# A fused attention and two-MLP kernel: the second MLP's combined weights are made during the first MLP

## The chip, the cores and the metric

The kernel runs on one core of a Trainium2 chip. The metric is the device time of one execution in microseconds (us), shown as the median of several runs. Five engines work in parallel and each takes its instructions in order: PE (matrix multiply, with its weight loads shown as PEld), DVE (vector), ACT (activations and copies), POOL (GpSimd) and SP, whose queue only issues DMAs here.

## The reference

```python
# decayed linear attention: B=4, H=8, S=768, D=48
state = alpha[:, :, t, :, None] * state + k[:, :, t] (outer) v[:, :, t]
y[:, :, t] = q[:, :, t] @ state
x = y as (3072 tokens, 384)
# first MLP, d_ff = 2048
x = silu(x @ w_in) @ w_out
# second MLP, d_ff = 1536
out = (silu(x @ w_gate) * (x @ w_val)) @ w_out2
```

Everything is float32. Weights arrive as 64-bit floats, and the kernel turns them into float32 itself: that is what `decode` does, with three integer operations on DVE (L47, L52, L57) on a tile of 128x384 words. A float32 product is formed as three PE products: each operand is split into a rounded high part (an ACT copy, `high_...`) and a low part (source minus high, `sub`, L267), and PE adds high*high, low*high and high*low.

## The kernel before

**First MLP with attention.** The 24 chunks of 128 tokens are put in seven blocks of 4, 3, 3, 3, 3, 4 and 4 chunks. For each block j the kernel runs 16 steps, one for each 128 rows of the hidden layer. A step has two half steps: `g1` makes the hidden row block (9 matmuls, L648 to L651), `act1` has ACT apply silu twice (L665, L666) and DVE form the low part `gl` (L267), and `g2` adds the row block's share of the output (9 matmuls, L682 to L685). `g1` of the next step is issued ahead of `g2` of this one. `slot` is called after each half step and interleaves the attention of the next block: `qkt` and `pt` for a pair of heads, `pv` for a finished chunk. At the end of a chunk's attention the rows go to the next block's input tile `x`, part of them by small DMAs (`rows_in`, L552), and at the end of a block `g2` stores the result `x1e` to DRAM (L694). Blocks 0 and 1 are interleaved; blocks 2 to 6 follow one another. In the profile block 2 begins at 200 us, block 6 at 483 us, and the first MLP ends at 546.4 us.

**Second MLP.** The 3072 tokens are three pairs of 512-token halves. For a pair, `group(p, u)` runs for u = 0..11 and multiplies 2x2 blocks with fewer products than the direct way: the moving operand is 9 prepared combinations of the tokens (`mov`, made by `moving_steps`), the stationary operand is 9 prepared combinations of four 128x128 weight blocks (`comb`, a high and a low half, 128 x 18 x 128 floats). A group has 33 matmuls (L827), and between them ACT copies (L861, L863, L876), silu (L842) and DVE additions and products (L867, L882, L845). Then the output stage of the pair runs: for each of 24 tiles `osplit` makes a high part on ACT and a low part `al` (DVE, and POOL for half of them in pair 0), and `og` issues 9 matmuls (L909) with the output weights `wo`.

**Making comb and wo.** One combined weight u takes two loads from DRAM (384 KB each, raw), two decodes (six DVE operations), four POOL operations on 128x128 (`combine`, L796 to L799), an ACT copy of 128x1152 (`high_comb`, L803), a POOL subtraction of 128x1152 (`low_comb`, L267) and a DMA store to `comb_d` (`keep_comb`, L810). Pairs 1 and 2 fetch it from there (`fetch_comb`, L814); pair 0 uses it where it was made. One wo takes one load, three DVE operations, an ACT copy (L818) and a POOL subtraction of 128x384. `units2` advances all of these by at most one item per stage; it is called from the last half steps of block 5, from most half steps of block 6, and inside pair 0 from the groups (`spare`, twice in even groups) and the output stage. A decode there is three DVE operations in a row.

**What sets the order.** The order on every queue is the order of the calls above. The tiles `big0`, `big1`, `big2` hold the blocks' inputs and results in turn.

Of the kernel before, what the change touches and what calls it, by code (L numbers as in the profile page):

```python
# [222 lines left out]
def fast(ctx, tc, pk, w1, w2, out, bad_i):  # L223
# [24 lines left out]
    mp = ctx.enter_context(tc.tile_pool(name="mp", bufs=2))  # L248

# [49 lines left out]
    def load_in(n, part=None):  # L299
# [416 lines left out]
    def moving_steps(p):  # L716
# [16 lines left out]
        def minus(out, x, y):  # L733
            POOL.tensor_tensor(out=out, in0=x, in1=y, op=ALU.subtract)
# [25 lines left out]
    f_t, comb_t, wo_t, loaded, ticks = {}, {}, {}, {}, [0]  # L760

    def comb_place(u):
        t = pools2["s"].tile([128, 18 * 128], F32R, tag=f"comb{u % 3}", name=f"comb{u}", bufs=1)
        comb_t[u] = t.rearrange("p (x i e) -> p x i e", x=2, i=9)
        return t
# [12 lines left out]
    def decode2(w):
        key = "2", w
        decode_unit(key, 0)  # L780
        decode_unit(key, 1)
        if w >= 2 * NF2:
            return decode_unit(key, 2)
        u, i = divmod(w, 2)
        if i == 0:
            f_t[u] = pools2["s"].tile([128, 10, 128], F32, tag="f", name=f"f{u}", bufs=2)
        to = f_t[u][:, 3 * (1 - i):3 * (1 - i) + 3].rearrange("p k e -> p (k e)")
# [13 lines left out]
    def high_comb(u):  # L801
        comb_place(u)
        ACT.activation(out=comb_t[u][:, 0], in_=f_t[u][:, 1:], func=AF.Copy)  # L803

    def low_comb(u):
        t = comb_t[u]
        sub(POOL, t[:, 1], f_t[u][:, 1:], t[:, 0])

    def keep_comb(u):
        SP.dma_start(out=comb_d[u], in_=comb_t[u].bitcast(F32).rearrange("p x i e -> p (x i e)"))  # L810

    def fetch_comb(u):
# [39 lines left out]
    def group(p, u, spare):  # L852
# [16 lines left out]
        if u % 2 == 0:  # L869
            spare()  # L870
# [23 lines left out]
    def osplit(p, f, b):  # L894
# [5 lines left out]
        sub(POOL if p == 0 and b else DVE, al, a, ah)  # L900
# [27 lines left out]
    st = dict.fromkeys(("a1", "a2", "a3", "b", "c", "gd", "qk", "pv", "end", "l1", "d1", "e1", "f1", "h1", "s1", "l2", "f2", "c2", "h2", "s2", "sp", "hw", "sw"), 0)  # L928
# [90 lines left out]
    def units2(room=3):  # L1019

        was = dict(st)
        ticks[0] += 1

        def step(key, limit, fn):
            if was[key] < limit:
                fn(st[key])
                st[key] += 1

        step("sp", was["s2"], keep_comb)
        step("s2", was["h2"], low_comb)  # L1030
        step("sw", was["hw"], low_wo)
        step("h2", min(was["c2"], room), high_comb)
        if "r" in pools2:
            step("hw", was["f2"] - NW, high_wo)
# [289 lines left out]
```

## Time and profile before

| | us |
|---|---|
| median of 3 runs | 1012.17 |
| lowest and highest run | 1011.71, 1014.96 |
| time of the profiled execution | 1011.36 |
| span of the profiled execution | 1009.6 |
| PE busy | 960.6 |
| DVE busy | 532.3 |
| ACT busy | 431.1 |
| POOL busy | 278.7 |

The span runs from the first to the last instruction; 1.76 us of the profiled time lie around it. Busy times are sums over an engine's instructions; a matmul's recorded duration overlaps with the next one's.

### The profile page before, as it was taken

The numbers are of one execution on the slowest core, as the hardware profiler recorded it, in microseconds if no ns is written. First come the engines' busy times: TensorE is split into PE (matmuls) and PEld (weight loads), VectorE is DVE, ScalarE is ACT, GpSimd is POOL, SyncE is SP. The second block draws the span as 40 slices with busy tenths as digits, with TensorE's granted clock in tenths as the row PEclk, the third lists the DMA queues.
The fourth block names the chain that finished last, engine by engine and source line by source line (L and its number), as shares of the span: only waits on it lengthen the run. The fifth ranks groups of instructions, "written<-read, shape, count | busy, mean of one in ns | idle before, by whom it ended". The sixth has DMA issues, their size and how long they took to land.

```text
span 1009.6 us, 14182 instructions
## 1 busy us (share of the span) xinstructions
PE 960.6 (95%) x5317; PEld 808.6 (80%) x5317; DVE 532.3 (53%) x912; ACT 431.1 (43%) x977; POOL 278.7 (28%) x347
## 2 busy tenths in 40 slices
PE   8889999999999999999999998879999999999995
PEld 5667798799999999888787776658788888788884
DVE  7889936444344453543842687793234354343432
ACT  3544435545454554452434444434343343433332
POOL 5344416423142342420630255374100020000000
PEclk9999999999999999999999999989999999999998
DMA  7763102322122222102820358460236410344001
GB/s 233 264 246 98 50 1 97 95 75 74 47 74 65 66 85 65 60 11 79 291 101 31 141 170 284 141 234 1 110 140 237 154 48 32 125 159 169 1 1 66
DMA packets 32780, 111.54 MB, mean 110 GB/s; under 512 B 3648, under 2 KB 7232, under 8 KB 28096
## 3 DMA queue, kind: packets, MB, share of 16 engines
q1 hardware_dynamic: 32224, 110.11, 31.8%
q8 instruction: 43, 0.70, 0.3%
q10 hardware_dynamic: 480, 0.46, 0.2%
q14 instruction: 33, 0.27, 0.1%
HBM read 85.00 MB, written 23.59 MB: 108 GB/s over the span
## 4 chain that ended last, share of the span: by engine, by line
PE 73%; DVE 13%; issue 5%; ACT 3%; POOL 3%; DMA 2%; SPq 0%; DVEq 0%; POOLq 0%; ACTq 0%
PE u L827 14%; PE o L909 13%; PE p L827 8%; PE h L648 5%; PE h L649 5%; PE h L651 5%; PE x L682 5%; PE x L683 5%; PE x L685 5%; DVE dec L47 3%; DVE raw L52 2%; PE y L489 2%; PE y L511 2%; POOL w L267 2%; DVE a L845 1%
## 5 line engine op out<-in xcount | busy, mean ns | idle before, releaser
L827 PE MATMUL u<-mov,comb 128*128 128x512 f32 x756 | 186.3, 392 | 12.5 <-ACT u L863 9.1
L827 PEld LDWEIGHTS u<-mov,comb 128*128 128x128 f32 x756 | 140.8, 188 | 47.4 <-ACT u L863 12.4
L909 PE MATMUL o<-ah,wo 128*128 128x512 f32 x432 | 136.4, 397 | 0.5 <-ACT ah L899 0.5
L267 DVE TENSOR_TENSOR gl<-h,gh 128x384 fp32r<-128x384 f32 (+1 forms) x112 | 68.6, 612 | 113.9 <-ACT h L666 110.7
L682 PE MATMUL x<-gh,w 128*128 128x384 f32 (+1 forms) x336 | 122.2, 364 | 2.5 <-ACT gh L665 2.5
L648 PE MATMUL h<-x,w 128*128 128x384 f32 (+1 forms) x336 | 122.9, 366 | 1.7 <-DMA x<-y 1.6
L683 PE MATMUL x<-gh,w 128*128 128x384 f32 (+1 forms) x336 | 121.4, 361 | 0.0
L665 ACT ACTIVATE gh<-h 128x384 fp32r<-128x384 f32 (+1 forms) x112 | 59.8, 534 | 144.4 <-PE h L651 144.0
L649 PE MATMUL h<-x,w 128*128 128x384 f32 (+1 forms) x336 | 121.1, 360 | 0.0
L827 PE MATMUL p<-mov,comb 128*128 128x512 f32 x432 | 111.9, 394 | 1.7 <-DVE a L845 1.7
L909 PEld LDWEIGHTS o<-ah,wo 128*128 128x128 f32 x432 | 83.2, 193 | 18.3 <-ACT ah L899 0.9
L827 PEld LDWEIGHTS p<-mov,comb 128*128 128x128 f32 x432 | 81.5, 189 | 20.2 <-DVE a L845 2.9
L909 PE MATMUL o<-al,wo 128*128 128x512 f32 x216 | 87.0, 403 | 7.7 <-DVE al L267 7.4
L685 PE MATMUL x<-gl,w 128*128 128x384 f32 (+1 forms) x336 | 85.5, 362 | 4.1 <-DVE gl L267 4.1
L651 PE MATMUL h<-x,w 128*128 128x384 f32 (+1 forms) x336 | 84.6, 360 | 0.0
L267 DVE TENSOR_TENSOR al<-a,ah 128x512 fp32r<-128x512 f32 x60 | 45.4, 757 | 70.6 <-ACT ah L899 68.2
L899 ACT ACTIVATE ah<-a 128x512 fp32r<-128x512 f32 x72 | 45.4, 630 | 82.4 <-PE o L909 73.8
L356 POOL TENSOR_TENSOR kq<-in,r 128x256 f32<-128x256 f32 x47 | 35.4, 753 | 156.2 <-DVE r L345 152.3
L682 PEld LDWEIGHTS x<-gh,w 128*128 128x128 f32 x336 | 63.5, 189 | 10.7 <-ACT gh L665 5.3
L685 PEld LDWEIGHTS x<-gl,w 128*128 128x128 f32 x336 | 60.7, 188 | 13.5 <-DVE gl L267 7.8
L648 PEld LDWEIGHTS h<-x,w 128*128 128x128 f32 x336 | 63.1, 188 | 10.5 <-issue 5.3
L458 DVE TENSOR_TENSOR pt<-s,mask 128x256 f32<-128x256 f32 x92 | 38.1, 418 | 60.3 <-PE s L435 59.1
(130 smaller groups left out, 1546.9 us busy)
## 6 DMA issues: line engine op xcount, KB each, us to landing
comb<-comb_d SPq DMA_DIRECT2D x24, 1152.0 KB, 5.1
raw<-in_w_dram SPq DMA_DIRECT2D x64, 384.0 KB, 4.8
in<-in_pk_dram SPq DMA_DIRECT2D x22, 770.5 KB, 4.2
comb_d<-comb SPq DMA_DIRECT2D x12, 1152.0 KB, 6.7
in_v<-in_pk_dram SPq DMA_DIRECT2D x24, 256.0 KB, 3.2
x1r<-x_d SPq DMA_DIRECT2D x6, 768.0 KB, 7.5
out_dram<-ob SPq DMA_DIRECT2D x18, 256.0 KB, 2.3
x_d<-x1e SPq DMA_DIRECT2D x4, 576.0 KB, 3.2
```

The source lines that it names most:

```text
L267: eng.tensor_tensor(out=lo, in0=src, in1=hi.bitcast(F32), op=ALU.subtract)
L458: DVE.tensor_tensor(out=pt, in0=s_t[g][0], in1=mask.rearrange("p (o t) -> p o t", o=1).to_broadcast([128, 2, C]), op=ALU.mult,)
L648: PE.matmul(acc, part(u, k), xh, start=(k == 0), stop=False)
L649: PE.matmul(acc, part(u, k, 1), xh, start=False, stop=False)
L651: PE.matmul(acc, part(u, k), xl, start=False, stop=(k == len(xk) - 1))
L665: ACT.activation(out=gh, in_=hb, func=AF.Silu)
L682: PE.matmul(x1_t[j][m], part(u, m), gh, start=(f == 0), stop=False)
L683: PE.matmul(x1_t[j][m], part(u, m, 1), gh, start=False, stop=False)
L685: PE.matmul(x1_t[j][m], part(u, m), gl, start=False, stop=(f == NF1 - 1))
L827: PE.matmul(acc, s[:, hs, i], x[:, hx], start=start and n == 0, stop=n == 2, skip_group_check=True,)
L899: ACT.activation(out=ah, in_=a, func=AF.Copy)
L909: PE.matmul(o_t[b][m], part(wo_t[f], m, l), x, start=(f == 0 and n == 0), stop=(f == NF2 - 1 and n == 2),)
```

## The change

The whole making of the combined weights leaves `units2` and goes to a new function `combs`, called in every half step of blocks 2 to 5. A counter gives one unit nine half steps: the six DVE decode operations one at a time in the first six, `combine` in the seventh, `high_comb` in the eighth, and the low part in three POOL operations of 128x384 in the ninth and in the first two of the next unit. The store follows two half steps later. One tile `fcomb` replaces two rotating `f` tiles, and `comb` is made in whichever of `big0` to `big2` the block leaves free, so one such tile is live at a time. All three pairs now fetch all twelve comb tiles from DRAM, the first three for pair 0 in block 6. What is left of `units2` is `units_o`, which only makes `wo`: three loads in block 6, then one call per group of pair 0. In `moving_steps` the four subtractions `minus` of a pair move from POOL to DVE, and in pair 0 the low parts `al` that POOL made move to DVE. Some padding of the attention tiles `in`, `r` and `g` is cut to make room. `start_phase2` moves by two half steps.

```diff
+    cw = ctx.enter_context(tc.tile_pool(name="cw", bufs=1))
+    raw2 = [cw.tile([128, 2 * DM], I32, name=f"raw2_{i}") for i in range(2)]
+    fcomb = cw.tile([128, 10, 128], F32, name="fcomb")
...
-            t = ap.tile([128, A_W + 2 * W + 123], F32, tag="in", name=f"in{n}")[:, :A_W + 2 * W]
+            t = ap.tile([128, A_W + 2 * W + 11], F32, tag="in", name=f"in{n}")[:, :A_W + 2 * W]
...
         def minus(out, x, y):
-            POOL.tensor_tensor(out=out, in0=x, in1=y, op=ALU.subtract)
+            DVE.tensor_tensor(out=out, in0=x, in1=y, op=ALU.subtract)
...
-    def low_comb(u):
-        t = comb_t[u]
-        sub(POOL, t[:, 1], f_t[u][:, 1:], t[:, 0])
+    def high_comb(u, j):
+        comb_view(u, big((0, 2, 1)[j % 3], f"comb{u}", F32R))
+        ACT.activation(out=comb_t[u][:, 0], in_=fcomb[:, 1:], func=AF.Copy)
+
+    def low_comb(u, k):
+        t, r = comb_t[u], slice(3 * k, 3 * k + 3)
+        sub(POOL, t[:, 1, r], fcomb[:, 1 + 3 * k:4 + 3 * k], t[:, 0, r])
...
+    def combs(j):
+
+        t, comb_tick[0] = comb_tick[0], comb_tick[0] + 1
+        u, k = divmod(t, 9)
+        if u > NF2 or (u == NF2 and k > 3):
+            return
+        if 0 < u:
+            if k < 2:
+                low_comb(u - 1, k + 1)
+            if k == 3:
+                keep_comb(u - 1)
+        if u == NF2:
+            return
+        if t == 0:
+            load2(0)
+            load2(1)
+        if k < 6:
+            decode2(2 * u + k // 3, k % 3)
+        if k in (3, 6) and u + 1 < NF2:
+            load2(2 * u + 2 + (k == 6))
+        if k == 6:
+            combine(u)
+        if k == 7:
+            high_comb(u, j)
+        if k == 8:
+            low_comb(u, 0)
...
-        sub(POOL if p == 0 and b else DVE, al, a, ah)
+        sub(DVE, al, a, ah)
...
+    def units_o():
 
         was = dict(st)
+        if st["sw"] < was["hw"]:
+            low_wo(st["sw"])
+            st["sw"] += 1
+        if st["hw"] < was["fw"]:
+            high_wo(st["hw"])
+            st["hw"] += 1
+        if st["fw"] < was["lw"]:
+            for i in range(3):
+                decode2(NW + st["fw"], i)
+            st["fw"] += 1
+        up_to("lw", min(st["lw"] + 1, st["sw"] + 3), lambda f: load2(NW + f), NF2)
...
-        if j == NB1 - 2 and hs > 26:
-            units2()
+        if 2 <= j < NB1 - 1:
+            combs(j)
...
-            if hs < 2 or hs % 3:
-                units2()
+            if hs in (3, 5, 7):
+                fetch_comb((hs - 3) // 2)
+            if hs in (9, 11, 13):
+                up_to("lw", st["lw"], lambda f: load2(NW + f), NF2)
...
-            if p == 0:
-                need2(u, u + 1)
-            group(p, u, (lambda: units2(u + 3)) if p == 0 else (lambda: None))
-            if p and u + 2 < NF2 and u:
+            group(p, u, units_o if p == 0 else (lambda: None))
+            if u + 2 < NF2 and u:
                 fetch_comb(u + 2)
```

How the queues change is seen at three places. On DVE, in groups 2 and 3 of pair 0 (u_0_2 and u_0_3 are the groups' additions, `dec`, `raw` and `f` a decode, `v` and `a` what the group goes on with), there stood before:

```order
L867 TENSOR_TENSOR u_0_2_5720<-u_0_2_5707,s_0_2_5705 128x512
L47 TENSOR_SCALAR dec_10_5725<-raw_5016 128x384
L52 SCALAR_TENSOR_TENSOR raw_5016<-raw_5016,dec_10_5725 128x384
L57 SCALAR_TENSOR_TENSOR f_5728<-raw_5016 128x384
L47 TENSOR_SCALAR dec_11_5733<-raw_5016 128x384
L52 SCALAR_TENSOR_TENSOR raw_5016<-raw_5016,dec_11_5733 128x384
L57 SCALAR_TENSOR_TENSOR f_5728<-raw_5016 128x384
L882 TENSOR_TENSOR v_2_5762<-u_0_2_5707,s_0_2_5705 128x512
L867 TENSOR_TENSOR u_0_3_5789<-u_0_3_5776,s_0_3_5774 128x512
L47 TENSOR_SCALAR dec_12_5796<-raw_5016 128x384
L52 SCALAR_TENSOR_TENSOR raw_5016<-raw_5016,dec_12_5796 128x384
L57 SCALAR_TENSOR_TENSOR f_5799<-raw_5016 128x384
```

And now, where L899, L912 and L877 are the lines that were L867, L882 and L845:

```order
L899 TENSOR_TENSOR u_0_2_5896<-u_0_2_5883,s_0_2_5881 128x512
L47 TENSOR_SCALAR dec_26_5901<-raw_2_5286 128x384
L52 SCALAR_TENSOR_TENSOR raw_2_5286<-raw_2_5286,dec_26_5901 128x384
L57 SCALAR_TENSOR_TENSOR raw_2_5286<-raw_2_5286 128x384
L912 TENSOR_TENSOR v_2_5930<-u_0_2_5883,s_0_2_5881 128x512
L899 TENSOR_TENSOR u_0_3_5959<-u_0_3_5946,s_0_3_5944 128x512
L47 TENSOR_SCALAR dec_27_5964<-raw_3_5287 128x384
L52 SCALAR_TENSOR_TENSOR raw_3_5287<-raw_3_5287,dec_27_5964 128x384
L57 SCALAR_TENSOR_TENSOR raw_3_5287<-raw_3_5287 128x384
L877 TENSOR_TENSOR a_2_0_5975<-p_0_3_5940,sg_2_0_5912 128x512
```

Three decodes in these two groups became two, one in each group, and they now decode output weights into their own raw tiles.

On ACT, in steps 9 to 11 of block 2 (`gh` and `h` are the two silu of a step, `kt`, `kh`, `qh` and `jk` attention), there stood before:

```order
L665 ACTIVATE gh_9_2601<-h_9_2587 128x384
L666 ACTIVATE h_9_2587<-h_9_2587 128x384
L467 ACTIVATE kt_99<-s_2597 128x2x48
L665 ACTIVATE gh_10_2641<-h_10_2627 128x384
L666 ACTIVATE h_10_2627<-h_10_2627 128x384
L467 ACTIVATE kt_100<-s_2637 128x2x48
L395 ACTIVATE kh_2655<-kq_2502 128x256
L397 ACTIVATE qh<-kq_2502 64x2x128 x2
L408 ACTIVATE jk,sums<-kq_2305 128x512
```

And now:

```order
L668 ACTIVATE gh_9_2643<-h_9_2629 128x384
L669 ACTIVATE h_9_2629<-h_9_2629 128x384
L470 ACTIVATE kt_105<-s_2639 128x2x48
L799 ACTIVATE comb_2660<-fcomb 128x1152
L668 ACTIVATE gh_10_2686<-h_10_2672 128x384
L669 ACTIVATE h_10_2672<-h_10_2672 128x384
L470 ACTIVATE kt_106<-s_2682 128x2x48
L398 ACTIVATE kh_2700<-kq_2533 128x256
L400 ACTIVATE qh<-kq_2533 64x2x128 x2
L411 ACTIVATE jk,sums<-kq_2320 128x512
L668 ACTIVATE gh_11_2733<-h_11_2719 128x384
```

The 128x1152 copy `comb` now stands between the silu of steps 9 and 10, behind the POOL operations that fill `fcomb`.

On SP, at the end of block 2 (`x<-y` are the rows that block 3 waits for, `x_d<-x1e` is block 2's result), there stood before:

```order
L310 DMA in_2458<-in_pk_dram 128x1541
L325 DMA in_v_2585<-in_pk_dram 128x512
L310 DMA in_2653<-in_pk_dram 128x1541
L325 DMA in_v_2780<-in_pk_dram 128x512
L552 DMA x_2383<-y_3_2384 16x2x384 x6
L694 DMA x_d<-x1e_2884 384x1x384
L310 DMA in_2958<-in_pk_dram 128x1541
```

And now:

```order
L619 DMA raw_1_88<-in_w_dram 128x768
L313 DMA in_2698<-in_pk_dram 128x1541
L809 DMA comb_d<-comb_2660 128x2304
L619 DMA raw_0_87<-in_w_dram 128x768
L328 DMA in_v_2836<-in_pk_dram 128x512
L555 DMA x_2405<-y_3_2406 16x2x384 x6
L619 DMA raw_1_88<-in_w_dram 128x768
L809 DMA comb_d<-comb_2874 128x2304
L619 DMA raw_0_87<-in_w_dram 128x768
L697 DMA x_d<-x1e_2959 384x1x384
```

A store of one combined weight and two raw loads now stand ahead of, and right behind, the six small DMAs.

## Rows read from the trace of the kernel before

**Rows 1.** The page: busy time of PE over the whole span.

```profile
PE 960.6 (95%) x5317; PEld 808.6 (80%) x5317; DVE 532.3 (53%) x912; ACT 431.1 (43%) x977; POOL 278.7 (28%) x347
```

**Rows 2.** Busy time by stretch: groups, then output stage, of each of three pairs.

```profile
core 0: us, PE busy (x) PEld busy (x) DVE busy (x) ACT busy (x) POOL busy (x), PEclk, DMA share, GB/s
546.40:652.00 105.60, 95.23 (x398) 74.50 (x397) 73.10 (x102) 46.67 (x75) 41.01 (x39) 0.98 0.52 183
652.00:715.40 63.40, 55.81 (x218) 43.07 (x217) 40.11 (x48) 24.47 (x43) 34.60 (x26) 0.92 0.30 104
715.40:807.30 91.90, 90.35 (x397) 73.85 (x396) 32.61 (x48) 35.89 (x63) 0.00 (x0) 1.00 0.47 169
807.30:857.00 49.70, 49.40 (x218) 40.59 (x217) 25.05 (x36) 20.43 (x34) 5.84 (x4) 1.00 0.11 38
```

**Rows 3.** Timeline of PE, instructions that waited (wait and releaser in brackets).

```profile
548.62 0.98 PE L827 MATMUL u<-mov,comb 128*128 128x512 f32 x3 [0.67 <-ACT u L863]
...
595.79 0.97 PE L827 MATMUL p<-mov,comb 128*128 128x512 f32 x3 [0.57 <-DVE a L845]
...
718.43 0.96 PE L827 MATMUL u<-mov,comb 128*128 128x512 f32 x3 [1.55 <-ACT u L863]
```

**Rows 4.** Timeline of DVE in an odd group: of pair 0, then of pair 1.

```profile
590.53 0.70 DVE L867 TENSOR_TENSOR u<-u,s 128x512 f32<-128x512 f32 x1 [2.76 <-PE u L827]
591.14 2.81 DVE L47 TENSOR_SCALAR dec<-raw 128x384 int32<-128x384 int32 x1
...
595.05 0.68 DVE L845 TENSOR_TENSOR a<-p,sg 128x512 f32<-128x512 f32 x1
...
727.20 0.70 DVE L867 TENSOR_TENSOR u<-u,s 128x512 f32<-128x512 f32 x1 [2.83 <-PE u L827]
728.52 0.69 DVE L845 TENSOR_TENSOR a<-p,sg 128x512 f32<-128x512 f32 x1 [0.62 <-PE p L827]
```

**Rows 5.** The operations on raw, comb and f: count, min/median/max ns; one combine.

```profile
L47 DVE TENSOR_SCALAR dec<-raw x64: 326/526/2831, 29.9 to 679.8; 128x384 int32<-128x384 int32 x64
L52 DVE SCALAR_TENSOR_TENSOR raw<-raw,dec x64: 526/559/1602, 36.3 to 681.3; 128x384 int32<-128x384 int32 x64
L57 DVE SCALAR_TENSOR_TENSOR f<-raw x24: 557/559/700, 478.7 to 629.9; 128x384 int32<-128x384 int32 x24
L267 POOL TENSOR_TENSOR wo<-raw,wo x12: 1027/1150/1477, 636.9 to 683.7; 128x384 fp32r<-128x384 f32 x12
L267 POOL TENSOR_TENSOR comb<-f,comb x12: 2666/2679/2987, 487.2 to 634.1; 128x1152 fp32r<-128x1152 f32 x12
571.57 0.46 POOL L797 TENSOR_TENSOR f<-f 128x128 f32<-128x128 f32 x1
```

**Rows 6.** Busy time by stretch: a dense early stretch, and blocks 2 to 5.

```profile
75.00:100.00 25.00, 23.56 (x114) 19.86 (x113) 24.66 (x38) 10.54 (x22) 11.91 (x11) 1.00 0.33 97
200.00:483.00 283.00, 282.93 (x1952) 261.86 (x1953) 122.21 (x278) 134.25 (x370) 82.67 (x128) 0.99 0.21 65
```

**Rows 7.** Timeline in block 6: ACT at a comb copy, PE just behind it.

```profile
499.19 1.17 ACT L803 ACTIVATE comb<-f 128x1152 fp32r<-128x1152 f32 x1 [4.37 <-POOL f L799]
...
500.89 0.50 PE L682 MATMUL x<-gh,w 128*128 128x512 f32 x1 [0.54 <-ACT gh L665]
```

**Rows 8.** DMAs, median us to landing; then SP and PE at two block ends.

```profile
comb<-comb_d SPq DMA_DIRECT2D x24, 1152.0 KB, 5.1
comb_d<-comb SPq DMA_DIRECT2D x12, 1152.0 KB, 6.7
x<-y SPq DMA_DIRECT2D x20, 48.0 KB, 2.1
...
258.63 3.80 SPq L552 DMA_DIRECT2D x<-y  x6
266.08 0.33 PE L648 MATMUL h<-x,w 128*128 128x384 f32 x1
...
199.96 0.41 PE L648 MATMUL h<-x,w 128*128 128x384 f32 x1 [1.59 <-DMA x<-y]
```

More of the change, by code (lines that the diff above doesn't have):

```diff
@@ L758, in moving_steps @@
         ]
[L760 to L765, printed above, removed]
+    comb_t, wo_t = {}, {}
     def w2_src(w):
-        if w >= 2 * NF2:
-            return w2[w - 2 * NF2, :, 2 * DM:]
+        if w >= NW:
+            return w2[w - NW, :, 2 * DM:]
         u, i = divmod(w, 2)
@@ L774, in load2, with decode2 @@
     def load2(w):
-        load_unit(("2", w), w2_src(w), pools2["raw"][:, w % 4])
-        loaded[w] = ticks[0]
-    def decode2(w):
+        load_unit(("2", w), w2_src(w), raw2[w % len(raw2)])
+    def decode2(w, step):
         key = "2", w
[L780 to L787, printed above, removed]
+        if step < 2 or w >= NW:
+            return decode_unit(key, step)
+        i = w % 2
+        to = fcomb[:, 3 * (1 - i):3 * (1 - i) + 3].rearrange("p k e -> p (k e)")
         raw = raw_t.pop(key)
@@ L809, in keep_comb, with comb_flat @@
+    def comb_flat(t):
+        return t.bitcast(F32).rearrange("p x i e -> p (x i e)")
     def keep_comb(u):
-        SP.dma_start(out=comb_d[u], in_=comb_t[u].bitcast(F32).rearrange("p x i e -> p (x i e)"))
+        SP.dma_start(out=comb_d[u], in_=comb_flat(comb_t.pop(u)))
     def fetch_comb(u):
-        t = comb_place(u)
-        SP.dma_start(out=t.bitcast(F32), in_=comb_d[u])
+        if u % 3 == 2:
+            t = big(1, f"comb{u}", F32R)
+        else:
+            t = pools2["s"].tile([128, 18 * 128], F32R, tag=f"comb{u % 3}", name=f"comb{u}", bufs=1)
+        comb_view(u, t)
+        SP.dma_start(out=comb_flat(comb_t[u]), in_=comb_d[u])
@@ L1017, in units1 @@
         up_to("l1", st["d1"] + ahead - 1, load1, NU1)
-    def units2(room=3):
+    def units_o():
         was = dict(st)
[L1022 to L1034, printed above, removed]
-        step("c2", min(was["f2"] // 2, NF2), combine)
-        w = st["f2"]
-        if w < st["l2"] and loaded[w] < ticks[0] - 1 and (w >= NW or w // 2 < st["s2"] + 2):
-            decode2(w)
-            st["f2"] += 1
-        free = st["f2"] if st["f2"] < NW else NW + st["sw"]
-        up_to("l2", min(st["l2"] + 1, free + 3), load2, NU2)
-    def need2(u, room):
-        while st["s2"] <= u:
-            units2(room)
+        if st["sw"] < was["hw"]:
[9 more added lines that the diff above has]
+        up_to("lw", min(st["lw"] + 1, st["sw"] + 3), lambda f: load2(NW + f), NF2)
     def need1(u):
@@ L1119, in start_phase2 @@
         pools2["s"] = ctx.enter_context(tc.tile_pool(name="sp2", bufs=2))
-        pools2["raw"] = big(1, "raw2", I32).rearrange("p (u c) -> p u c", u=4)
+        assert comb_tick[0] > 9 * NF2 + 3
+        for i in range(2, 4):
+            raw2.append(pools2["s"].tile([128, 2 * DM], I32, name=f"raw2_{i}", bufs=1))
         small = mp.tile([128, 2 * 512], F32, tag="y3", name="small", bufs=1)
```

29 lines of the change are left out of this document (14 added, 15 removed).

## The prediction

> **What bounds the kernel now.** I read the totals first. PE is busy for 960.6 of 1009.6 us [rows 1], so the end is set by PE's work plus PE's idle time, and only a change of one of these counts. PE's matmuls stay as they are, so the question is where PE idles or runs slowly. The busy time by stretch answers it: blocks 2 to 5 of the first MLP (200 to 483 us) have PE busy for 282.93 of 283.00 us [rows 6], so nothing can be won there. The three pairs of the second MLP have the same matmuls. Pair 1 takes 91.90 us for its groups and 49.70 us for its output stage, 141.6 us; pair 0 takes 105.60 and 63.40 us, 169.0 us [rows 2]. Pair 0 is the one that makes combined and output weights while it runs: its DVE is busy 73.10 us in the groups against 32.61 us in pair 1, and POOL 41.01 against 0. Its granted clock is also lower, 0.98 and 0.92 of the full 2.4 GHz against 1.00, so part of its output stage ran at the lower level of 1.2 GHz; the lengths of the stretches contain that.
>
> The timeline of DVE then shows the mechanism. In an odd group of pair 0 the group's addition starts at 590.53 us, a decode operation (L47) holds DVE for 2.81 us, and the next product `a` starts only at 595.05 us, 4.52 us after the addition; in pair 1 the same distance is 1.32 us (727.20 to 728.52) [rows 4]. DVE is 3.2 us later than it need be, and PE then waits 0.57 us at 595.79 for `a` [rows 3]. So 3.2 us of delay cost 0.57 us: a group has some 2.6 us to spare on DVE.
>
> **Removed from pair 0: 28.3 us.** If pair 0 ran like pair 1 it would take 141.6 us, 27.4 us less. It begins with a wait of 0.67 us where pair 1 begins with 1.55 us, because pair 1's first ACT copies queue behind the eviction of an output [rows 3]; pair 0 has no such output ahead of it and keeps that 0.88 us. Together 28.3 us. Pair 0 now has to fetch its comb tiles as pair 1 does; a fetch of 1152 KB lands in 5.1 us [rows 8] and a group lasts 91.9 / 12 = 7.7 us, with three tiles in turn, so pair 1's pace holds.
>
> **What stays in pair 0: 0.5 us.** One output weight per group: three DVE operations of 0.33, 0.56 and 0.56 us, 1.45 us [rows 5], plus an ACT copy and one POOL subtraction of 1.15 us. In pair 1 DVE idles 0.62 us before `a` [rows 4], so 1.45 us make `a` some 0.8 us late, or 2.0 us if the first operation also waits out the whole POOL subtraction. Both lie under the 2.6 us to spare. Bounds: nothing, and 12 x 0.54 = 6.5 us if each group still loses what the odd group loses now, rounded down. I take 0.5 us, near the lower bound, since the delay fits. The twelve low parts and four subtractions that come to DVE in an output stage that has 25.05 of 49.70 us busy in pair 1 [rows 2] are hidden by its idle time: the steps there take 49.70 / 24 = 2.1 us of PE, and without that idle time each operation would cost what it lasts, about 0.7 us.
>
> **Block 6: 0.5 us won.** There PE waits 0.54 us once, behind an ACT that had waited 4.37 us for POOL's `combine` before a comb copy [rows 7]. The copies leave block 6. Bounds: 0 to 0.54 us, and I take 0.5 us.
>
> **Added to blocks 2 to 5: 3.6 us lost.** This is the term that no row shows directly. Each of 12 units adds six DVE operations, 2 x 1.45 = 2.9 us, four combines of 0.46 us and three low parts of 1.15 us on POOL, 5.3 us (I use the 128x384 form of `wo`, since the old 128x1152 of 2.68 us is cut in three) [rows 5], and one ACT copy of 1.17 us [rows 7]. In all: DVE 34.8, POOL 63.5, ACT 14.0 us over 283 us. The shares rise on DVE from 122.21 to 157 us (43% to 55%), on POOL from 82.67 to 146 us (29% to 52%), on ACT from 134.25 to 148 us (47% to 52%) [rows 6]. No engine is full, but queues are in order, and a small operation may stand ahead of one that PE needs. Lower bound: nothing. Upper bound: the dense early stretch, where DVE is at 98.6% with decodes among attention and PE loses 1.44 of 25 us, 5.8% [rows 6]; over 283 us that is 16.3 us. Between the ends I go by DVE's share: (55.4 - 43.2) / (98.6 - 43.2) = 0.22 of 5.76%, 1.27%, 3.6 us.
>
> The Trainium skill, page "SBUF — State Buffer", section "Who interferes with whom", speaks against this step: it says that VectorE and GpSimd share one pair of SBUF ports, taken as an exclusive lock for a whole instruction, so that a VectorE tensor_scalar, or an operation with two SBUF inputs, blocks behind a GpSimd operation that reads SBUF. The trace agrees: L47 takes 0.33 us alone and up to 2.83 us beside a POOL low part of 2.68 us [rows 5]. By that rule POOL's 63.5 us count against DVE as well, which is the second rival below; by the rows alone the sum has 3.6 us here.
>
> **Queues that the moved step passes.** SP gets 24 loads and 12 stores among the attention loads and the small `x<-y` DMAs. At the end of block 2 the last of six `x<-y` is issued by 262.43 us and lands about 2.1 us later, 264.5 us; PE wants it at 266.08 us: 1.5 us to spare [rows 8]. A store (6.7 us to landing) and a load are ahead of them in SP's queue at two of the four block ends, some half steps earlier; I count nothing, and price the miss below. The comb copy on ACT waits for the previous unit's store, since there is one tile: it is four half steps behind it, 4 x 66/32 = 8.2 us in block 2 by 200 to 266 us [rows 8], and the store lands after 6.7 us. What is queued behind the copy on ACT is the next silu, which PE needs. The cut padding of `in`, `r` and `g` changes no shape; no row shows an effect of addresses, and I count nothing.
>
> **The sum.** 1011.36 (the profiled execution; 0.8 us under the median of the runs, 1012.17) - 28.3 + 0.5 - 0.5 + 3.6 = 986.7 us.
>
> **The rivals.**
> First, as above: 986.7 us; own range 982.6 (no loss in blocks 2 to 5, none in pair 0) to 990, half way to the second. Chance 0.63.
>
> Second, DVE and POOL hinder each other in blocks 2 to 5 as if each of POOL's added microseconds took DVE's time too. DVE's share is then (157 + 63.5) / 283 = 78%, and the interpolation gives 0.63 of 5.76%, 10.2 us: 993.3 us, up to the dense stretch's 16.3 us, 999.4 us. For it: the 2.81 us of rows 4. Against it: in block 6 one unit after another was made, with PE losing 0.54 us in all [rows 7]. Chance 0.20.
>
> Third, the output weights keep their price in pair 0, 6.5 us: 992.7 us. For it: output stage 63.40 us against 49.70 us [rows 2], where only they and the next pair's operands are made. Against it: there two or three engines' work met in 2.1 us steps, now it is one unit in 7.7 us. Chance 0.06.
>
> Fourth, `x<-y` lands behind a store at two block ends. Each costs the store's 6.7 us less 1.5 us, and up to 2.8 us of slow clock by estimate (PE waited 1.59 us for `x<-y` at 199.96, and the granted clock of 200 to 483 us is 0.99, 1% of 283 us short [rows 6, 8]): 2 x 8.0 = 16.0 us, 1002.7 us. Chance 0.04.
>
> Fifth, it becomes slower: the comb copy waits on ACT for the store of the unit before it and holds the silu. A wait of 4.37 us cost PE 0.54 us [rows 7], so about 3.8 us are free. To pass 1014.4 us, 27.7 us more than my sum, each of the 12 waits would have to reach 3.8 + 2.3 = 6.1 us, so a store would have to land after 8.2 + 6.1 = 14.3 us where 6.7 us is the median. It decides from there. Chance 0.04.
>
> Sixth, the change doesn't do what it says: the fetches for pair 0 come late, and what it no longer makes it waits for. That needs 28 us / 12 = 2.3 us per group, a landing of some 15 us with fetches issued two groups ahead, against 5.1 us [rows 8]. About 1011 us. Chance 0.03.
>
> **How the numbers follow.** The predicted time is the first case's, 986.7 us. The range runs from 981.5, one microsecond below the first case's bound for the rounding of the stretches, to 997 us, which takes in the third case and most of the second; it leaves out the fourth to the sixth and the end of the second, under 2 in 10. What a measurement of this kernel can tell from no change is about 0.3%, 3 us. Slower holds the fifth case, 0.04; same the sixth, 0.03; all the others are faster, 0.93.
>
> **What would show it.** Right: pair 0's groups take about 92 us and its output stage about 50 us, at a granted clock of 1.00; no wait of PE for `a`; blocks 2 to 5 take 284 to 290 us. The second case is seen in L47, L52 and L57 well over 0.56 us in blocks 2 to 5 and PE waiting for `gl` or `pt`; the fourth in PE waiting for `x<-y` at 266, 330, 398 and 477 us or so; the fifth in ACT waiting at the comb copy for a DMA or for POOL, with PE waiting for `gh`. My sum is wrong if blocks 2 to 5 lose more than 10 us, or if pair 0 stays above 150 us.

## The result, and the profile after

The changed kernel took 984.57 us, the median of 4 runs (983.55 to 985.72); the kernel before, on the same chip, took 1011.94 us (1010.81 to 1014.96, 4 runs). The ratio is 0.9725 with a 95% interval of 0.9701 to 0.975: faster, by 27.4 us. The profiled execution took 984.02 us with a span of 982.2 us, where the forecast, made against the profiled execution before, was 986.7 us.

On the page, PE's busy time fell by 9.6 us against [rows 1] while the span fell by 27.4 us, so most of the gain is idle time of PE that has gone. The page's first part:

```profile
span 982.2 us, 14200 instructions
PE 951.0 (97%) x5317; PEld 806.4 (82%) x5317; DVE 528.2 (54%) x936; ACT 430.6 (44%) x977; POOL 257.3 (26%) x347
```

Busy time by stretch of the changed kernel, groups and output stage of pair 0 and then of pair 1, to be laid beside [rows 2]. The columns are the stretch, its length, each engine's busy time with its count, the granted clock, the DMAs' share and GB/s:

```profile
core 0: us, PE busy (x) PEld busy (x) DVE busy (x) ACT busy (x) POOL busy (x), PEclk, DMA share, GB/s
549.20:640.20 91.00, 90.33 (x398) 74.00 (x397) 52.16 (x84) 40.79 (x74) 11.32 (x11) 1.00 0.57 208
640.20:689.80 49.60, 49.30 (x217) 40.37 (x216) 26.73 (x40) 20.88 (x35) 1.03 (x1) 1.00 0.10 37
689.80:781.60 91.80, 90.18 (x397) 74.00 (x396) 32.88 (x48) 35.88 (x63) 0.00 (x0) 1.00 0.47 170
781.60:831.20 49.60, 49.30 (x218) 40.47 (x217) 26.04 (x40) 20.43 (x34) 0.00 (x0) 1.00 0.10 38
```

Pair 0 takes 91.00 + 49.60 = 140.6 us where it took 169.0, and it now reads like pair 1. PE's idle time fell by 9.7 us in the groups (10.37 less 0.67) and by 7.3 us in the output stage (7.59 less 0.30). The other 11.4 us are PE's busy time. The granted clock was 0.98 and 0.92 and is now 1.00, the full 2.4 GHz, which by 90.33 / 0.98 and 49.30 / 0.92 us accounts for 6.1 us of them, an estimate. Most of the other 5.3 us go with the waits, by estimate, since a wait here costs PE more than its own length. In block 4, further down, waits of 0.58, 0.74, 0.39 and 0.26 us make their steps 0.85, 1.03, 0.67 and 0.56 us longer, about 0.28 us more each. Pair 0 had 19 waits of PE over 0.15 us and has two now; 17 x 0.28 is 4.8 us.

The timeline of PE, the instructions that still waited in pair 0, and the first of pair 1:

```profile
551.41 0.98 PE L859 MATMUL u<-mov,comb 128*128 128x512 f32 x3 [0.67 <-ACT u L895]
641.08 0.50 PE L939 MATMUL o<-al,wo 128*128 128x512 f32 x1 [0.30 <-DVE al L270]
692.97 0.96 PE L859 MATMUL u<-mov,comb 128*128 128x512 f32 x3 [1.62 <-ACT u L895]
```

No wait for `a` is left. The waits at the starts of the two pairs are close to those of [rows 3]: 0.67 and 1.62 us, where the sum had 0.67 and 1.55. The timeline of DVE in an odd group of pair 0, which answers to [rows 4]:

```profile
560.07 0.70 DVE L899 TENSOR_TENSOR u<-u,s 128x512 f32<-128x512 f32 x1 [2.83 <-PE u L859]
560.67 0.94 DVE L47 TENSOR_SCALAR dec<-raw 128x384 int32<-128x384 int32 x1
561.65 0.56 DVE L52 SCALAR_TENSOR_TENSOR raw<-raw,dec 128x384 int32<-128x384 int32 x1
562.25 0.56 DVE L57 SCALAR_TENSOR_TENSOR raw<-raw 128x384 int32<-128x384 int32 x1
562.72 0.68 DVE L877 TENSOR_TENSOR a<-p,sg 128x512 f32<-128x512 f32 x1
```

From the addition to `a` it is 2.65 us, where it was 4.52 us, and 1.32 us in pair 1. The output weight's three operations make `a` 1.3 us late, and PE does not notice. All twelve output weights are made this way now, one per group, as the low parts' first and last starts show:

```profile
L270 POOL TENSOR_TENSOR wo<-raw,wo x12: 1020/1031/1036, 560.4 to 641.6; 128x384 fp32r<-128x384 f32 x12
```

Before, they were made from 636.9 to 683.7 us, ten of the twelve low parts in the output stage from 652 us on, while the last low part of a combined weight starts at 634.1 us [rows 5]. What left the output stage, besides the operations that changed engine, is therefore the making of output weights, and what left the groups is the making of combined weights.

The price is in blocks 2 to 5. I took the start of each step (its first `h<-x,w` matmul) from both traces and subtracted; a step "loses" the time by which its start falls further behind. By these starts blocks 2 to 5 end at 477.76 us before and at 481.43 us now; the 483 us of [rows 6] lie in block 6 already. At the start of block 2 the changed kernel is 0.15 us ahead, at the end of block 5 it is 3.67 us behind, so blocks 2 to 5 lose 3.82 us; step 6 of block 6 gains 0.86 us. Of the loss, 3.43 us lie in five steps (counted from 0): step 9 of block 3 with 0.32 us, and in block 4 steps 4, 5, 7 and 13 with 0.85, 1.03, 0.67 and 0.56 us. The rest is about 0.01 us in many steps. PE's waits in block 4:

```profile
343.02 0.43 PE L436 MATMUL s<-qh,kh 128*128 128x352 f32 x1 [0.58 <-ACT kt L470]
352.33 0.43 PE L436 MATMUL s<-qh,kh 128*128 128x352 f32 x1 [0.74 <-ACT kt L470]
358.61 0.43 PE L436 MATMUL s<-qh,kh 128*128 128x352 f32 x1 [0.39 <-ACT kt L470]
387.03 0.43 PE L436 MATMUL s<-qh,kh 128*128 128x352 f32 x1 [0.26 <-ACT kt L470]
```

PE waits for `kt`, an attention copy on ACT. What makes it late at 343, at 358 and at 387 is the order on DVE. The same step on DVE, before and then after, and ACT's copy after:

```profile
340.16 0.56 DVE L267 TENSOR_TENSOR gl<-h,gh 128x384 fp32r<-128x384 f32 x1 [2.26 <-ACT h L666]
340.63 0.41 DVE L458 TENSOR_TENSOR pt<-s,mask 128x256 f32<-128x256 f32 x1
...
341.32 0.56 DVE L270 TENSOR_TENSOR gl<-h,gh 128x384 fp32r<-128x384 f32 x1 [0.86 <-ACT h L669]
341.80 0.55 DVE L47 TENSOR_SCALAR dec<-raw 128x384 int32<-128x384 int32 x1
342.27 0.41 DVE L461 TENSOR_TENSOR pt<-s,mask 128x256 f32<-128x256 f32 x1
...
342.71 0.25 ACT L470 ACTIVATE kt<-s 128x96 f32<-128x96 f32 x1 [1.42 <-DVE pt L461]
```

The step's first matmul is at 340.23 us before and at 340.68 us now, so `gl` starts 0.7 us later in the step, and `pt` 1.2 us later, since a decode operation (L47) now stands between them. `kt` waits for `pt`, and PE for `kt`. At 357.33 and 385.81 us the same decode stands between `gl` and `pt`, with 0.61 and 0.56 us. A decode ahead of `pt` is not enough by itself: in block 2 one stands there eight times, and PE waits at none of them.

The shares of the engines do not tell where this happens. Windows of the changed kernel: steps 4 to 11 of block 2, where PE has no idle time; most of block 4; and blocks 2 to 5 with the first 4 us of block 6.

```profile
216.00:250.00 34.00, 34.00 (x266) 33.02 (x265) 24.66 (x50) 19.66 (x54) 23.55 (x34) 1.00 0.45 148
...
333.00:402.00 69.00, 67.03 (x516) 63.54 (x515) 46.45 (x99) 38.44 (x110) 51.41 (x66) 1.00 0.51 173
...
199.80:485.00 285.20, 283.09 (x1944) 260.81 (x1945) 166.48 (x344) 145.18 (x380) 156.09 (x212) 0.99 0.42 140
```

POOL is busy 75% of that stretch of block 4 and DVE 67%. In the stretch of block 2 it is 69% and 73%, without a wait of PE; over all it is 55% and 58%. At 352 it is something else, which the forecast did not contain. The timeline of ACT:

```profile
349.70 0.49 ACT L542 ACTIVATE x<-y 128x384 fp32r<-128x384 f32 x1 [2.98 <-DMA comb_d<-comb]
```

The copy of an attention row into `x`, the tile that feeds the next block, waits 2.98 us for a *store of a combined weight*. Unit 6's combined weight lies in the same large buffer (`big0`) that becomes the next block's `x`, and its store was issued only at 341.41 and landed 8.2 us later, the slowest of the twelve:

```profile
341.41 0.42 SPq L809 DMA_DIRECT2D comb_d<-comb  x1
```

ACT takes its work in order, so the `kt` copies queue behind this one, and PE waits for `kt`. The rows of operations and DMAs that answer to [rows 5 and 8], by tile (count, then min/median/max ns) and, in the last two, by DMA (KB and median us to landing):

```profile
L47 DVE TENSOR_SCALAR dec<-raw x64: 329/588/1079, 28.9 to 635.6; 128x384 int32<-128x384 int32 x64
L57 DVE SCALAR_TENSOR_TENSOR fcomb<-raw x24: 521/548/1305, 213.8 to 429.8; 128x384 int32<-128x384 int32 x24
L270 POOL TENSOR_TENSOR comb<-fcomb,comb x36: 990/1014/2196, 228.2 to 444.9; 128x384 fp32r<-128x384 f32 x36
...
comb<-comb_d SPq DMA_DIRECT2D x36, 1152.0 KB, 5.1
comb_d<-comb SPq DMA_DIRECT2D x12, 1152.0 KB, 5.6
```

Decodes and low parts have medians near those of [rows 5] and long single ones, up to 2.2 us on POOL: two engines that hinder each other in places, and not throughout.

### The profile page after: what moved, and what is told of

Same layout as the page of the kernel before. It is cut to its first block, busy times and chain, and to the rows that moved or that the text cites. A ratio compares the mean times of both kernels' runs of the same rounds, so it can differ in the third digit from the quotient of the medians.

```text
span 982.2 us, 14200 instructions
## 1 busy us (share of the span) xinstructions
PE 951.0 (97%) x5317; PEld 806.4 (82%) x5317; DVE 528.2 (54%) x936; ACT 430.6 (44%) x977; POOL 257.3 (26%) x347
## 4 chain that ended last, share of the span: by engine, by line
PE 81%; DVE 6%; issue 4%; ACT 3%; DMA 2%; POOL 2%; SPq 0%; POOLq 0%; DVEq 0%; ACTq 0%
PE u L859 17%; PE o L939 15%; PE p L859 10%; PE h L651 6%; PE h L652 5%; PE h L654 5%; PE x L688 5%; PE x L685 5%; PE x L686 5%; PE y L492 2%; PE y L514 2%; POOL w L270 2%; PE s L436 1%; DVE dec L47 1%; PE s L438 1%
## 5 line engine op out<-in xcount | busy, mean ns | idle before, releaser
L859 PE MATMUL u<-mov,comb 128*128 128x512 f32 x756 | 183.8, 390 | 3.8 <-ACT u L895 3.8
L939 PE MATMUL o<-ah,wo 128*128 128x512 f32 x432 | 133.1, 389 | 0.0
L859 PE MATMUL p<-mov,comb 128*128 128x512 f32 x432 | 109.7, 389 | 0.0
L939 PEld LDWEIGHTS o<-ah,wo 128*128 128x128 f32 x432 | 81.1, 188 | 16.7
L270 DVE TENSOR_TENSOR al<-a,ah 128x512 fp32r<-128x512 f32 x72 | 50.6, 703 | 71.6 <-ACT ah L929 68.4
L939 PE MATMUL o<-al,wo 128*128 128x512 f32 x216 | 84.5, 391 | 0.9 <-DVE al L270 0.9
L651 PEld LDWEIGHTS h<-x,w 128*128 128x128 f32 x336 | 63.2, 188 | 10.4 <-issue 5.3
L685 PEld LDWEIGHTS x<-gh,w 128*128 128x128 f32 x336 | 63.5, 189 | 9.7 <-ACT gh L668 4.4
L686 PEld LDWEIGHTS x<-gh,w 128*128 128x128 f32 x336 | 63.4, 189 | 5.1
L652 PEld LDWEIGHTS h<-x,w 128*128 128x128 f32 x336 | 63.3, 188 | 5.1
```

What stands on the lines that cost most here:

```text
L270: eng.tensor_tensor(out=lo, in0=src, in1=hi.bitcast(F32), op=ALU.subtract)
L651: PE.matmul(acc, part(u, k), xh, start=(k == 0), stop=False)
L652: PE.matmul(acc, part(u, k, 1), xh, start=False, stop=False)
L685: PE.matmul(x1_t[j][m], part(u, m), gh, start=(f == 0), stop=False)
L686: PE.matmul(x1_t[j][m], part(u, m, 1), gh, start=False, stop=False)
L859: PE.matmul(acc, s[:, hs, i], x[:, hx], start=start and n == 0, stop=n == 2, skip_group_check=True,)
```

## The experiments

Two questions were open. First, why is pair 0 faster? My theory, called A in the expectations: because the making of the combined weights has left it. Rivals: the low parts and subtractions that the change moves from POOL to DVE do part of it (B); or the making was dear only for its form, one long POOL operation of 2.68 us (theory C), and cutting it in three would do as well. Second, where do the 3.8 us of blocks 2 to 5 come from: crowding on DVE and POOL (F), the store that holds a block's input tile (theory E), or something other than the making (D)? Each run is compared with the kernel before; "loses" is the loss over blocks 2 to 5 by the starts of the steps, 3.82 us in the changed kernel.

**The engine moves undone in the changed kernel** (undo_engines).

```diff
-            DVE.tensor_tensor(out=out, in0=x, in1=y, op=ALU.subtract)
+            POOL.tensor_tensor(out=out, in0=x, in1=y, op=ALU.subtract)
...
-        sub(DVE, al, a, ah)
+        sub(POOL if p == 0 and b else DVE, al, a, ah)
```

> The changed kernel with the four subtractions `minus` and pair 0's low parts `al` back on POOL. Theory A (the gain is that the combined weights are no longer made in pair 0; the engine moves add nothing): within 2 us of 984.6 us, pair 0 still 140 to 142 us. Rival B (the engine moves bring a part of the gain): 988 us or more, with PE waiting for `al` or `mov` in the output stage of pair 0.

Measured: 983.69 us (982.92 to 984.38), ratio 0.9728 (0.9707 to 0.975). The same time, and pair 0 has the same two waits of PE, 0.67 and 0.30 us. Blocks 2 to 5 lose 3.58 us. The moves add nothing once the making has left, and rival B falls.

**The engine moves alone, in the kernel before** (before_dve): the same two lines, the other way round.

> The kernel before with `minus` and pair 0's `al` on DVE and nothing else changed. Theory A: no gain worth speaking of, 1006 to 1014 us, since DVE is the crowded engine in pair 0's output stage (40.11 of 63.40 us). Rival B: 1004 us or less.

Measured: 1006.65 us (1003.26 to 1007.89, 10 runs) beside 1010.6 us, ratio 0.9952 (0.9936 to 0.9967). They are worth some 0.5% by themselves, as long as the making is there to be relieved: pair 0 is 2.5 us shorter in its trace, with the clock of its output stage at 0.97 where it was 0.92 [rows 2]. The largest of PE's waits in that stage stays (timeline of PE, this kernel):

```profile
679.80 0.50 PE L909 MATMUL o<-al,wo 128*128 128x512 f32 x1 [3.04 <-DVE al L267]
```

So the 28 us aren't the moves', and what these are worth alone isn't added to them.

**The long low part cut in three, in the kernel before** (before_thirds).

```diff
-        sub(POOL, t[:, 1], f_t[u][:, 1:], t[:, 0])
+        for k in range(3):
+            r = slice(3 * k, 3 * k + 3)
+            sub(POOL, t[:, 1, r], f_t[u][:, 1 + 3 * k:4 + 3 * k], t[:, 0, r])
```

> The kernel before with the one low part of 128x1152 of each combined weight cut into three POOL operations of 128x384 and nothing else changed. Theory A (it is the amount of work in pair 0): at most a third of the gain, 1002 to 1011 us. Rival C (it is that one POOL operation holds DVE's decode for 2.7 us): most of the gain of pair 0's groups, 995 to 1000 us, and L47 no longer above 1.3 us.

Measured: 1010.84 us (1006.69 to 1011.96), ratio 0.9992 (0.9977 to 1.0006): no gain. The timeline of DVE in an odd group of pair 0 tells why:

```profile
592.47 1.14 DVE L47 TENSOR_SCALAR dec<-raw 128x384 int32<-128x384 int32 x1
593.64 1.26 DVE L52 SCALAR_TENSOR_TENSOR raw<-raw,dec 128x384 int32<-128x384 int32 x1
594.93 1.25 DVE L57 SCALAR_TENSOR_TENSOR f<-raw 128x384 int32<-128x384 int32 x1
```

L47 no longer takes 2.81 us as in [rows 4], but now all three decodes stretch to some 1.2 us beside POOL's three parts (3.39 us together). From the addition at 591.86 to `a` at 596.11 it is 4.25 us, after 4.52. The pieces together hold DVE nearly as long as the one operation did. The groups of pair 0 become 1.2 us shorter in this trace (105.6 to 104.3 us) and step 6 of block 6 loses 1.0 us, so theory C accounts for little of the 14.6 us that the groups have gained, and for none of the time. The Trainium skill, page "SBUF — State Buffer", section "Who interferes with whom", says that the port pair which the two engines share is an exclusive lock. The rows agree: L47 lasts 2.81 us beside POOL's one operation of 2.68 us [rows 4 and 5], and here each of the three decodes lasts about as long as one of POOL's three parts (3.39 / 3 = 1.13 us).

**One combined weight made and stored, and fetched for all twelve** (one_unit). The other eleven units' making is left out.

```diff
-        SP.dma_start(out=comb_flat(comb_t[u]), in_=comb_d[u])
+        SP.dma_start(out=comb_flat(comb_t[u]), in_=comb_d[0])
...
-        if u > NF2 or (u == NF2 and k > 3):
+        if u > 1 or (u == 1 and k > 3):
```

(and the loads and the unit count in the same way)

> The changed kernel with only combined weight 0 made and stored, and that one fetched for all twelve (the other eleven are left out, so the second MLP computes with the wrong weights). Theory A (blocks 2 to 5 lose 3.8 us to the making): 980 to 981 us, with the steps of blocks 3 and 4 as long as in the kernel before. Rival D (the 3.8 us come from something else, the cut padding or the moved start of phase 2): 984 us.

Measured: 980.81 us (979.57 to 982.09), ratio 0.9698 (0.9677 to 0.9719); it loses 0.6 us, in no step over 0.1 us. The making costs 3.82 - 0.6 = 3.2 us in blocks 2 to 5; the 0.6 us that stay are what D could account for.

**A pause of the making around the end of block 3** (pause), so that unit 6 lies in another large buffer and its store does not hold the next `x`.

```diff
-        if 2 <= j < NB1 - 1:
+        if 2 <= j < NB1 - 1 and not (j == 3 and hs > 28) and not (j == 4 and hs < 3):
```

> The changed kernel with the making of combined weights halted in the last three half steps of block 3 and the first three of block 4, so that unit 6 lies in big2 instead of big0, where block 5's input goes. Theory E (in block 4 ACT is held because the first rows of block 5's input wait for unit 6's store out of the same tile: 2.98 us at 346.7 us): step 5 of block 4 loses nothing instead of 1.0 us, and blocks 2 to 5 lose 2.2 to 2.8 us instead of 3.8. Rival F (all of the loss is DVE and POOL crowded by the added work): the loss of step 5 comes back in another step, 3.5 us or more in all.

Measured: 981.35 us (979.93 to 983.64), ratio 0.9698 (0.9667 to 0.9728); it loses 1.65 us, and the waits of ACT for `comb_d` are gone. Steps 4 and 5 of block 4 lose nothing now; step 9 of block 3 (0.32 us), steps 7 and 10 of block 4 (0.66 and 0.14 us) do. That is less than theory E gave, since the pause also moves the decodes: in steps 4 and 13 of block 4 `pt` now follows `gl` at once, while in step 7 a decode stands between them.

**The making halted in every second of the first 24 half steps of block 4** (thin), which thins the crowd and delays stores.

```diff
-        if 2 <= j < NB1 - 1:
+        if 2 <= j < NB1 - 1 and not (j == 4 and hs < 24 and hs % 2 == 0):
```

> The changed kernel with the making halted in every second of the first 24 half steps of block 4, so that block 4 gets two thirds of its added work less and unit 6's store is issued three half steps later. Rival F (crowding): block 4 loses under 1 us instead of 3.3, some 2 us faster than the changed kernel. Theory E (the tile): ACT waits longer for that store, 5 us or more, and block 4 loses more than 3.3 us; 1 to 4 us slower than the changed kernel.

Measured: 989.38 us (988.55 to 990.98), ratio 0.9787 (0.9757 to 0.9817): 4.8 us above the changed kernel. It loses 8.75 us, of which 4.74 in step 5 of block 4. The waits of this kernel (engine, line, what it waited for: us in all, count, longest):

```profile
ACT comb L799 <- DMA comb_d<-comb: 7.8, 2, 5.4
...
ACT x L542 <- DMA comb_d<-comb: 5.9, 1, 5.9
```

The store is issued at 345.59 us in place of 341.41, and the same copy into `x` now waits 5.9 us in place of 3.0. Fewer operations and a longer time: the tile, not the crowd, sets step 5. Steps 4, 7 and 13 lose nothing; there, too, no decode stands between `gl` and `pt`. Three other steps lose 3.2 us together, 1.02 of them in step 6, behind PE's wait of 4.04 us, with a granted clock of 0.98 over 333 to 402 us (1.00 in the changed kernel), and 1.47 in step 1 of block 5, where the ACT comb copy waits 5.4 us for a store and PE then 1.19 us for `gh`.

**Low parts filled with zeros by a POOL memset** (low_memset; from unit 1 on the low part is left out).

```diff
-        sub(POOL, t[:, 1, r], fcomb[:, 1 + 3 * k:4 + 3 * k], t[:, 0, r])
+        if u < 1:
+            sub(POOL, t[:, 1, r], fcomb[:, 1 + 3 * k:4 + 3 * k], t[:, 0, r])
+        else:
+            POOL.memset(t[:, 1, r].bitcast(F32), 0.0)
```

> The changed kernel with POOL filling the low parts of combined weights 1 to 11 with zeros instead of subtracting (the low part of the second MLP's weights is left out). Rival F: with 20 us or more less on POOL and none of these operations reading the tiles that DVE reads, blocks 2 to 5 lose under 1 us. Theory E: step 5 of block 4 still loses 0.7 us or more, the other steps nothing; 1 us in all.

Measured: 983.72 us (980.19 to 984.44), ratio 0.9716 (0.9681 to 0.975). By the time alone no difference from the changed kernel; by the steps it loses 2.04 us in place of 3.82. Step 5 of block 4 loses nothing though ACT still waits 2.0 us for the store, so about that much is covered; step 4 goes from 0.85 to 0.49 us and step 7 from 0.67 to 0.24; step 9 of block 3 and step 13 of block 4 stay at 0.32 and 0.56. In step 13 the decode still stands between `gl` and `pt`. The low parts carry some of the loss, and neither expectation had the split.

**Low parts on DVE** (low_dve): `sub(DVE, ...)` in the same line.

> The changed kernel with the low parts of the combined weights subtracted on DVE instead of POOL, 36 operations of about 0.55 us. If POOL is the crowded engine of block 4, blocks 2 to 5 lose 1 to 2.5 us; if DVE is, they lose 5 us or more, with PE waiting for `gl` and `kt` in blocks 3 and 4.

Measured: 984.66 us (984.18 to 986.3), ratio 0.9738 (0.9707 to 0.9768); it loses 4.43 us. Step 4 of block 4 goes to 1.39 and step 13 to 1.15 us, while step 5 loses nothing with a wait of 1.9 us for the store. By these steps DVE's queue is the more sensitive of the two, but the result lies between the expectations and the time is the changed kernel's.

**The store issued one half step earlier** (early_keep): `if k == 3` becomes `if k == 2` ahead of `keep_comb`.

> The changed kernel with each combined weight's store issued one half step earlier, right behind its last low part. Theory E (unit 6's store holds the tile that block 5's first rows need): ACT's wait for it falls from 2.98 us to under 2 us, step 5 of block 4 loses under 0.3 us instead of 1.0, and the other late steps (9 of block 3, 4, 7 and 13 of block 4) stay. Rival F (crowding alone): no step changes by more than 0.2 us.

Measured: 984.82 us (981.42 to 985.41), ratio 0.9737 (0.9715 to 0.9759). The wait for the store is 2.6 us in place of 3.0, and step 5 loses 0.66 us in place of 1.03; the other steps of blocks 3 and 4 stay. The timeline of SP's queue in this kernel shows that the edit did not move the store:

```profile
338.56 0.33 SPq L313 DMA_DIRECT2D in<-in_pk_dram  x1
338.94 0.42 SPq L809 DMA_DIRECT2D comb_d<-comb  x1
```

The program is some 2.5 us further here than in the changed kernel: unit 6's last low part starts at 336.18 us, there at 338.64. The store follows 2.76 us after it, there 2.77 us. In both it stands right behind an attention load that had held SP's queue. So this run does not test theory E, and its 0.37 us in step 5 are within what one and the same code shows: undo_engines, too, loses 0.67 us there. Over blocks 2 to 5 this run loses 1.99 us, since step 1 of block 2 is 1.6 us shorter in it; the last section shows why.

**The pause, and the combine one half step earlier** (pause_c5): `if k == 6` becomes `if k == 5` in front of `combine`, on top of the pause.

> The paused version, with `combine` issued one half step earlier, so that ACT's comb copy does not come right behind it. If the 0.32 us that step 9 of block 3 lost in every version so far come from ACT waiting for `combine` (2.10 us there), that step loses under 0.1 us, and the time is that of the paused version or up to 0.5 us less. If they come from DVE and POOL slowing each other, the step stays.

Measured: 982.19 us (980.63 to 982.96), ratio 0.9705 (0.9686 to 0.9724). The loss in step 9 of block 3 is gone, so it was ACT's comb copy that waited for POOL's `combine`; the loss of 0.68 us in step 7 of block 4 stays. It loses 1.40 us, and the time cannot be told from the pause's.

**The pause, and the making halted in five more half steps of block 4** (pause_thin).

```diff
-        if 2 <= j < NB1 - 1:
+        rest = (j == 3 and hs > 28) or (j == 4 and (hs < 3 or hs in (4, 8, 12, 16, 20)))
+        if 2 <= j < NB1 - 1 and not rest:
```

> The paused version, with the making halted in five more half steps of block 4 (4, 8, 12, 16, 20), now that unit 6's store is out of the way. If what is left of the loss in block 4 (0.9 us of late steps) is crowding, it falls under 0.3 us and the time is 0.5 to 1 us under the paused version's; if not, the same.

Measured: 981.03 us (979.74 to 981.72), ratio 0.9695 (0.9676 to 0.9715). It loses 0.82 us, of which 0.34 in step 9 of block 3, and no step of block 4 over 0.1. All work of the making is still done. Windows of pause and then of this kernel, same columns as above:

```profile
333.00:402.00 69.00, 68.62 (x527) 65.69 (x526) 42.86 (x95) 38.11 (x109) 43.17 (x59) 1.00 0.49 161
...
333.00:402.00 69.00, 69.00 (x531) 66.65 (x530) 42.45 (x91) 38.96 (x110) 43.97 (x57) 1.00 0.41 136
```

POOL is at 43.97 of 69 us, 64% in place of the changed kernel's 75%, and PE at 69.00 of 69.00. But pause has POOL at 43.17 us in the same stretch and still loses 0.66 us in step 7, so the share is not what takes the loss away. The timeline of DVE in step 7, pause and then pause_thin:

```profile
355.69 0.56 DVE L270 TENSOR_TENSOR gl<-h,gh 128x384 fp32r<-128x384 f32 x1 [0.86 <-ACT h L669]
356.17 0.56 DVE L47 TENSOR_SCALAR dec<-raw 128x384 int32<-128x384 int32 x1
356.65 0.41 DVE L461 TENSOR_TENSOR pt<-s,mask 128x256 f32<-128x256 f32 x1
...
355.25 0.56 DVE L270 TENSOR_TENSOR gl<-h,gh 128x384 fp32r<-128x384 f32 x1 [0.86 <-ACT h L669]
355.73 0.41 DVE L461 TENSOR_TENSOR pt<-s,mask 128x256 f32<-128x256 f32 x1
```

The decode is gone from between `gl` and `pt`, and PE's wait for `kt`, 0.38 us in pause, with it. What the expectation called crowding is thus the place of single operations in DVE's queue; no run moves one decode alone. This is the lowest ratio measured, 0.9695 against the changed kernel's 0.9725; the intervals overlap, so the 3 us between them (0.3% of 1011 us) rest on the steps more than on the times.

## Why the prediction was right

The class, the time and, for pair 0, the mechanism were as forecast: 986.7 us against 984.0 us for the profiled execution, within the first case's own range. By the steps of the sum:

**Pair 0, -28.3 and +0.5 us.** Measured -28.4 us in all, so the residue of the output weights in the groups is nothing measurable. The argument was that an output weight makes `a` 0.8 to 2.0 us late and that a group has 2.6 us to spare; `a` came 1.3 us late and PE did not wait. The first operation waited out part of the POOL subtraction (L47 0.94 us). That neither the engine moves nor the form of the low part is the cause was shown by undo_engines, before_dve and before_thirds together. For the groups this leaves the making of the combined weights. For the output stage, 13.8 of the 28.4 us, it leaves it only indirectly: no combined weight was made there any more [rows 5], and what left it is the output weights' making, which now has room in the groups, one unit in each. No run spreads the output weights over the groups while the combined weights are still made there, so the two shares are not separated. The third rival (6.5 us kept) is out, and so is the sixth: twelve fetches more, and PE waits for none of them in pair 0.

**Block 6, -0.5 us.** It gained 0.86 us. PE's one wait of 0.54 us [rows 7] understated what the step had lost, as waits do in pair 0 and block 4.

**Blocks 2 to 5, +3.6 us.** Measured +3.82 us, and the making's part of it 3.2 us. The size is right, the picture only half. The forecast spread a loss evenly over 283 us by DVE's share, and the shares came out near the forecast: DVE 58% (forecast 55%), POOL 55% (52%), ACT 51% (52%). The loss in fact stands in five steps, four of them in block 4. The prediction's own argument, that a small operation may stand ahead of one that PE needs, is what happens in three of them, where a decode stands ahead of `pt`. In a fourth it is the ACT comb copy, which waits for `combine`. A share doesn't say where such an order hurts: in block 2 PE loses nothing at 69% of POOL and 73% of DVE, and pause and pause_thin differ at the same share. So it is luck that the interpolation by a share came so close. In step 5 another mechanism adds 1.03 us, a store that holds the buffer which the next block's `x` is to be written into. I had checked the comb tile's reuse by the next comb copy, and not that the large buffers have other users. thin shows what this is worth where it is worse: 4.74 us in one step.

**The second rival** (10.2 to 16.3 us) falls, though its rule holds for single operations: L57 takes up to 1.30 us beside a low part of 1.40 us, a low part up to 2.20 us beside three DVE operations, and before_thirds shows DVE losing POOL's time in pieces too. In blocks 2 to 5 nearly all of this fits into idle time of the two engines.

**The fourth and fifth rivals.** No wait of PE for `x<-y` at any end of blocks 2 to 5, so the 1.5 us to spare in SP's queue held. The comb copy waited for a store once, 2.4 us, below the 3.8 us that I had called free; the store of 5.6 us landed sooner than the 6.7 of [rows 8]. The fifth rival named the right resource, a store that ACT waits for, at the wrong instruction; its own chain is seen in thin alone, where the comb copy waits 5.4 us and PE 1.19 us for `gh`.

**Not in the sum:** pair 2 and the tail are 1.6 us shorter (152.6 to 151.0 us to the end), of which 0.7 us is a shorter wait at its start (2.25 to 1.54 us); pair 1 gains 0.2 us. Together with the terms above these make up the 2.7 us that the forecast was too high. That the 1.6 us are the change's is not shown. Pair 2's groups take 92.4 us in the profile before and 91.7 us now, but also 91.8 us in before_thirds, which is the kernel before at that place; and from its output stage to the end it is 60.2 us before, 59.3 us now, and 59.7 to 60.6 us in the nine experiments on the changed kernel. What the 0.01 us per step are, which are lost with one unit too, stays open; the cut padding of `in`, `r` and `g` was not tried alone.

## What to carry to other kernels

Work that starves PE in one stage may be moved into a stage whose engines have room, but that room is to be read step by step and queue by queue: the loss appears where a moved operation stands ahead of one that PE waits for and that is late already. Neither a mean share nor a peak of it shows the place. For each buffer that a moved step borrows, list everyone who writes it next and when the DMA that reads it lands; a store behind which an in-order engine waits can cost more in one step (4.74 us in thin) than all the added arithmetic did in four blocks. And cutting a long operation in pieces helps little if the other engine loses nearly the same time to the pieces.

## What the hardware showed unexpectedly

The granted clock after one and the same wait is not always the same. At the start of block 2 PE waits 1.59 us for `x<-y` [rows 8]. In the profiles of the kernel before, the changed kernel and ten experiments the granted clock of the stretch from 200 to 206 us is 0.72 or 0.73, which lies between the levels of 1.2 and 2.4 GHz; in early_keep, whose program is the same up to there, it is 1.00. The thin kernel starts from the same wait at the same time: its first matmul after 1.59 us of waiting is at 198.88 us, that of early_keep, after 1.59 us, at 198.83. The windows of early_keep, then of thin:

```profile
200.00:206.00 6.00, 6.00 (x33) 5.61 (x33) 2.00 (x4) 3.08 (x7) 0.00 (x0) 1.00 0.26 93
```

```profile
200.00:206.00 6.00, 6.00 (x23) 5.38 (x23) 1.25 (x2) 1.96 (x4) 0.00 (x0) 0.72 0.12 34
```

33 matmuls against 23 in the same 6 us, and step 1 of block 2 is 1.6 us shorter in early_keep than in the kernel before. That is half of the 3 us between the changed kernel and pause_thin, so a single execution says little about differences of that size. What decides the level after the wait stays open.
